# Nineteen products of the unit matrix with itself, ahead of four waits of TensorE in the first chunk of a state-space and gated feed-forward kernel

## The chip, the cores and the metric

The kernel runs on one core of a Trainium2 chip. The metric is the device time of one execution in microseconds (us). Before the change it is 373.65 us, the median of three runs (373.58 to 373.71).

## What is computed

A chunked state-space recurrence ("attention" part) gives a matrix of 3072 rows and 256 columns, and a gated feed-forward layer follows it.

```python
# attention part, per chunk of the sequence (4 batches, 8 heads, 768 positions, 32 channels, state 16)
cum = np.cumsum(la, axis=-1)                      # la: log of the clipped decays a
L = np.exp(cum[:, :, :, None] - cum[:, :, None, :]) * causal
CB = np.einsum('bhin,bhjn->bhij', Cc, Bc)
y_intra = np.einsum('bhij,bhjd->bhid', CB * L, xc)
y_inter = np.einsum('bhin,bhnd->bhid', Cc, state) * np.exp(cum)[:, :, :, None]
y[:, :, sl] = y_intra + y_inter
state = decay_full[:, :, None, None] * state + np.sum(Bx, axis=2)
# feed-forward part, on y as rows of 256
gate = 1.0 / (1.0 + np.exp(-(x @ w_gate)))        # 256 -> 1536
val = x @ w_val
out = (gate * val) @ w_out                        # 1536 -> 256
```

## The kernel before

**Tiling and stages.** The sequence of 768 positions is cut into six chunks of 128 (`NCH`), and a unit is one chunk of one of the four batches (`Unit`, and `FirstUnit` for the first chunk). A unit transposes B and C on TensorE with the unit matrix `eye` (tile `pt`, L386 and L387), takes scores of C with B (`pcb`, L464), weighs them with decays on VectorE (`m`, L478), multiplies by x (L490) and by B for the states (L497), and adds the part that comes from earlier states (L541; L624 in the first chunk). The decays of the first chunk are spread over partitions by TensorE (tile `pa`, L580) and become products along the row by a scan on VectorE (L586). When the four batches of a chunk are done, the feed-forward layer takes them together as 512 columns: gate products (`pg`), a sigmoid on ScalarE (`g`), value products (`pv`), gate times value on VectorE (`h`), then the output projection (`po`, L839 to L859). In the first chunk the first four pairs of gate and value are done in halves of 256 columns (L714), so that they can start when half of the rows exist; two more use whole float32 weights (L804). All others use weights and inputs split into a high and a low part (L813).

**Weights.** Each weight tile `wr` arrives by DMA (L304, L308) and is put into its working form by VectorE, ScalarE, VectorE, ScalarE and GpSimd in turn (`split_w`, L318 to L331).

**What sets the order.** Nothing reorders the work when the program runs: each engine's order is written out beforehand by `run()`. It keeps a list of tasks, each a generator that yields one step at a time with an engine, a cost and what it needs and makes, and picks the next step by planned starting times and by the due times of the table `DUES`. When a step is picked, the generator goes on and issues that step's instructions. On the chip each engine works through its list and waits on semaphores where its operands are not there yet. All DMAs are issued by SyncE in one order, over eight semaphore lanes in turn (`LANES = 8`), so that a transfer also waits for the one eight places ahead of it.

**The PSUM banks.** The pool `ps_mm` has three buffers of the tag `mm`, taken in turn by every tile of that tag: `pa`, `pp`, `pg`, `pv`, `po`. A tile can be written when the reader of the tile three places earlier is done.

**The start.** L126 multiplies a zero tile three times (`WARM`) before any input is there. Behind it stand the spreads `pa` of the first units, the transposes of unit 0_0 (which wait for a part of B and C), `pp`, the rest of the spreads and scores, then the transposes of 0_2 and 0_3 (the second half of the first chunk's positions), the products L490 and L497, and the first gate product `pg0_0_0`. The step names that the change uses are `products0_0`, `products0_2`, `products0_3` (L993) and `gate0_0_0` (L1023).

Of the kernel before, what the change touches and what calls it, by code (L numbers as in the profile page):

```python
# [8 lines left out]
F32 = mybir.dt.float32  # L9
# [49 lines left out]
AHEAD = 46.7  # L59
STATE = 30.0  # L60
SPARE = 1.0


W_MAX = (2.0 - 2.0**-3 - 2.0**-23) * 2.0**16
# [3 lines left out]
def tile_ssd_then_gated_ffn(  # L68
# [11 lines left out]
    nc = tc.nc  # L80
# [4 lines left out]
    P = 128  # L85
# [23 lines left out]
    ps_mm = ctx.enter_context(tc.tile_pool(name="ps_mm", bufs=3, space=PSUM))  # L109
# [20 lines left out]
    eye = const.tile([P, P], F32, name="eye")  # L130
# [34 lines left out]
    tasks = []  # L165
# [14 lines left out]
    def run():  # L180

        free = {"sp": 1.0, "pe": 1.2 + 1.7 * WARM, "act": 3.5, "dve": 6.0, "pool": 6.2, "none": 0.0}
        port_free = [0.0]
        dma_free = 0.0
        landed = [0.0] * LANES

        turns, turn_of = [0.0] * 3, {}
        made = {}
        spare = {"y": [0.0], "banks": [0.0] * 3, "cb": [0.0], "g": [0.0] * 3, "o": [0.0] * 2}
        tasks.sort(key=lambda t: t[:2])  # L190
        while tasks:
            ready_ones = []
            for n, (_, _, (eng, cost, needs, makes, port, buffers), ready, gen, name) in enumerate(tasks[:400]):
                if any(k not in made for k in needs) or any(m > len(spare[k]) for k, m in buffers.items()):
                    continue
                if buffers.get("banks") == 1:
                    if turns[-3] is None:
                        continue
                    ready = max(ready, turns[-3])
                for k, m in buffers.items():  # L200
                    ready = max([ready] + spare[k][: max(m, 0)])

                def begin(e):
                    s = max([free[e], ready] + [made[k][0] for k in needs if made[k][1] != e or e == "sp"])
                    return max(s, port_free[0]) if e == "pool" or (e == "dve" and port) else s

                if not isinstance(eng, str):
                    cost, eng = min(zip(cost, eng), key=lambda ce: begin(ce[1]) + ce[0] + SPARE * (ce[1] == "dve"))
                ready_ones.append((begin(eng), eng, n, cost))
            if not ready_ones:  # L210
                raise ValueError(f"the plan has a circle: {[t[2] for t in tasks[:20]]}")
            first = min(ready_ones, key=lambda r: r[0])

            start, eng, n, cost = next(r for r in ready_ones if r[1] == first[1] and r[0] <= first[0] + HOLD)
            t = tasks[n]
            _, _, needs, makes, port, buffers = t[2]
            end = start + cost
            if eng == "sp":

                many, end = round(cost / 0.52), start  # L220
                for _ in range(many):
                    end = max(end, landed[-LANES]) + 0.52
                    dma_free = max(dma_free, end + DMA_L) + port / many
                    landed.append(dma_free + DMA_L)
            free[eng] = end
            if eng == "pool" or (eng == "dve" and port):
                port_free[0] = end
            t[3] = end + {"pe": PE_L}.get(eng, SEM)
            if eng == "sp":
                t[3] = landed[-1]  # L230
            for k in makes:
                made[k] = t[3], eng
            if buffers.get("banks") == 1:
                turn_of[t[5]] = len(turns)
                turns.append(None)
            elif buffers.get("banks") == -1:
                turns[turn_of.pop(t[5])] = t[3]
            for k, m in buffers.items():
                spare[k] = sorted(spare[k][max(m, 0) :] + [t[3]] * -m)
            try:  # L240
                t[2] = t[4].send(eng)
            except StopIteration:
                del tasks[n]
# [774 lines left out]
    for k in range(NCH):  # L1018
# [16 lines left out]
        if k == 0:  # L1035
            t = FFN1
    run()


# [29 lines left out]
```

## Time and profile before

| what | us |
|---|---|
| median of three runs | 373.65 |
| the profiled execution | 374.85 |
| its span, from the first to the last instruction | 373.0 |
| TensorE busy in it | 360.9 |
| VectorE, ScalarE, GpSimd busy in it | 157.0, 151.1, 150.1 |

The profiled execution is one run of its own: 373.0 us of span and 1.85 us around it. The traces are read with times from the start of that span. PE is TensorE's matmuls and PEld its weight loads, which overlap them; DVE is VectorE, ACT ScalarE, POOL GpSimd, and SP or SPq SyncE, which issues the transfers. A row of the timeline merges like instructions that follow each other: start, time from the first's start to the last's end, engine, line, operation, output and inputs, count; in brackets the idle time before it and what ended that.

### The profile page before, as it was taken

What the parts mean: (1) busy time and instruction counts of PE and PEld (TensorE: products, weight loads), DVE (VectorE), ACT (ScalarE), POOL (GpSimd) and SP (SyncE); (2) the same over time, 40 slices, a digit from 0 to 9 for tenths busy, and PEclk for the clock granted to TensorE, in tenths of its full rate; (3) what the DMA queues carried; (4) which work ended last, traced back from release to release, by engine and by line L of the source; (5) the groups of instructions that cost most, each with busy time, mean ns of one, the idle gap of its engine ahead of it and who ended that gap; (6) DMA issues with size and microseconds to landing.
All of it is one profiled execution on the core that took longest, in us unless ns stands there. A gap on an engine that the chain in (4) does not pass through costs nothing.

```text
span 373.0 us, 8123 instructions
## 1 busy us (share of the span) xinstructions
PE 360.9 (97%) x3376; PEld 287.0 (77%) x3376; DVE 157.0 (42%) x277; ACT 151.1 (41%) x314; POOL 150.1 (40%) x159
## 2 busy tenths in 40 slices
PE   7788999999999999999999999999999999999996
PEld 2267668877878888888878888788877788888885
DVE  4756557768435444553354622430224440222201
ACT  2656686423575411544511245430254420254400
POOL 4425476463797520244440045430144420145410
PEclk9669999999999999999999999999999999999999
DMA  6999996527236322502332300400000000000000
GB/s 121 208 233 184 243 314 169 96 44 122 67 30 113 30 71 60 106 22 34 26 99 82 89 4 6 53 10 29 30 1 2 2 2 28 30 0 0 2 28 28
DMA packets 89270, 26.27 MB, mean 70 GB/s; under 512 B 76306, under 2 KB 82002, under 8 KB 89234
## 3 DMA queue, kind: packets, MB, share of 16 engines
q1 hardware_dynamic: 89234, 25.76, 31.8%
q8 instruction: 26, 0.43, 0.5%
q14 instruction: 10, 0.08, 0.1%
HBM read 22.41 MB, written 3.34 MB: 69 GB/s over the span
## 4 chain that ended last, share of the span: by engine, by line
PE 88%; SPq 5%; DMA 4%; POOL 1%; issue 1%; DVE 0%; ACT 0%
PE pv L813 25%; PE pg L813 24%; PE po L850 15%; PE po L851 7%; PE po L839 6%; DMA cn<-in_C_dram 2%; SPq L304 2%; PE pcb L464 2%; PE pcb L490 2%; PE pcb L541 2%; SPq L262 1%; DMA bn<-in_B_dram 1%; SPq L274 1%; PE pcb L497 1%; POOL wr L331 1%; PE pt L386 1%
## 5 line engine op out<-in xcount | busy, mean ns | idle before, releaser
L781 POOL TENSOR_TENSOR h<-g,h 128x512 fp32r<-128x512 f32 x60 | 78.5, 1308 | 126.6 <-ACT h L779 126.3
L813 PE MATMUL pv<-xh,w 128*128 128x512 f32 x264 | 93.9, 396 | 0.0
L813 PE MATMUL pg<-xh,w 128*128 128x512 f32 x264 | 93.3, 394 | 0.0
L850 PE MATMUL po<-w,h 128*128 128x512 f32 x228 | 82.1, 402 | 0.0
L775 DVE TENSOR_TENSOR g<-pv,g 128x512 f32<-128x512 f32 x60 | 41.5, 691 | 93.0 <-PE pv L813 87.5
L779 ACT CAST h<-g 128x512 fp32r<-128x512 f32 x59 | 36.6, 621 | 75.7 <-DVE g L775 75.7
L851 PE MATMUL po<-w,h 128*128 128x256 f32 x228 | 63.9, 280 | 0.0
L813 PEld LDWEIGHTS pg<-xh,w 128*128 128x128 f32 x264 | 49.6, 188 | 10.8 <-issue 0.2
L813 PEld LDWEIGHTS pv<-xh,w 128*128 128x128 f32 x264 | 49.6, 188 | 10.7 <-issue 0.3
L813 PE MATMUL pv<-xl,w 128*128 128x512 f32 x132 | 51.5, 390 | 0.0
L813 PE MATMUL pg<-xl,w 128*128 128x512 f32 x132 | 51.4, 390 | 0.0
L850 PEld LDWEIGHTS po<-w,h 128*128 128x128 f32 x228 | 42.8, 188 | 11.0 <-issue 0.5
L754 ACT ACTIVATE g<-pg 128x512 f32<-128x512 f32 x68 | 40.7, 599 | 14.7 <-PE pg L813 13.8
L851 PEld LDWEIGHTS po<-w,h 128*128 128x128 f32 x228 | 43.0, 189 | 0.2
L866 ACT COPY o<-po 128x256 f32<-128x256 f32 x20 | 7.5, 373 | 65.7 <-PE po L851 65.1
L419 DVE TENSOR_TENSOR_SCAN ab<-ab,delta 128x512 f32<-128x512 f32 x20 | 28.0, 1406 | 8.3 <-DMA ab<-a_z 8.2
L868 DVE TENSOR_TENSOR o<-po,o 128x256 f32<-128x256 f32 x20 | 8.4, 424 | 49.6 <-ACT o L866 49.5
L813 PEld LDWEIGHTS pg<-xl,w 128*128 128x128 f32 x132 | 24.8, 188 | 4.8
L813 PEld LDWEIGHTS pv<-xl,w 128*128 128x128 f32 x132 | 24.8, 188 | 4.6
L348 POOL TENSOR_TENSOR w<-wr,w 128x512 fp32r<-128x512 f32 x18 | 23.8, 1326 | 9.7 <-ACT w L346 8.8
L331 POOL TENSOR_TENSOR wr<-wr 128x512 int32<-128x512 int32 x18 | 19.6, 1091 | 20.0 <-ACT wr L329 17.9
L839 PE MATMUL po<-wr,h 128*128 128x256 f32 x96 | 23.4, 393 | 0.0
(96 smaller groups left out, 371.1 us busy)
## 6 DMA issues: line engine op xcount, KB each, us to landing
ab<-a_z SPq DMA_DIRECT2D x40, 128.0 KB
wr<-in_moe_w_val_dram SPq DMA_DIRECT2D x6, 512.0 KB
wr<-in_moe_w_gate_dram SPq DMA_DIRECT2D x6, 512.0 KB
wr<-in_moe_w_out_dram SPq DMA_DIRECT2D x6, 512.0 KB
out_dram<-o SPq DMA_DIRECT2D x24, 128.0 KB
xn<-in_x_dram SPq DMA_DIRECT2D x10, 256.0 KB
bn<-in_B_dram SPq DMA_DIRECT2D x10, 128.0 KB
cn<-in_C_dram SPq DMA_DIRECT2D x10, 128.0 KB
```

The costliest lines, as they stand in the source:

```text
L331: nc.gpsimd.tensor_tensor(out=lw.bitcast(I32), in0=hw.bitcast(I32), in1=lw.bitcast(I32), op=ALU.add)
L348: engines[eng].tensor_tensor(out=lo, in0=lw, in1=hi.bitcast(F32), op=ALU.subtract)
L419: nc.vector.tensor_tensor_scan(out=t.rearrange("p h l -> p (h l)"), data0=t.rearrange("p h l -> p (h l)"), data1=delta.rearrange("p h l -> ...
L754: nc.scalar.activation(gs[k, f], pm, AF.Sigmoid)
L775: nc.vector.tensor_tensor(out=g, in0=pm, in1=g, op=ALU.mult)
L779: copies[eng](hh, g)
L781: engines[eng].tensor_tensor(out=hl, in0=g, in1=hh.bitcast(F32), op=ALU.subtract)
L813: nc.tensor.matmul(pm, w[:, part, kt, fs], xx[:, kt], start=(i == 0), stop=(i == 3 * NK - 1))
L839: nc.tensor.matmul(acc[:, :DM], hs[k, f][:, js], whole[NF + f // 2][:, f % 2], start=start, stop=stop, skip_group_check=True,)
L850: nc.tensor.matmul(acc, hh, w.rearrange("p i m -> p (i m)"), start=start, stop=False, skip_group_check=True)
L851: nc.tensor.matmul(acc[:, :DM], hl, w[:, 0, :], start=False, stop=stop, skip_group_check=True)
L868: nc.vector.tensor_tensor(out=o, in0=acc[:, DM:], in1=o, op=ALU.add)
```

## The change

A table `FILLS` names four steps of TensorE in the first chunk. When `run()` has picked one of them, and before its instructions are issued, a tile `fill` of the pool `ps_mm` is taken and the unit matrix is multiplied by itself into its first 128 columns: 5, 6, 3 and 5 times, 19 in all. Nothing reads `fill`.

```diff
+FILLS = {"products0_0": {0: 5}, "products0_2": {0: 6}, "products0_3": {0: 3}, "gate0_0_0": {0: 5}}
...
+        nth = {}
+
+        def warm_up(many):
+
+            if many:
+                fill = ps_mm.tile([P, 512], F32, tag="mm", name="fill")
+            for _ in range(many):
+                nc.tensor.matmul(fill[:, :P], eye, eye, start=True, stop=True)
+
         tasks.sort(key=lambda t: t[:2])
...
             start, eng, n, cost = next(r for r in ready_ones if r[1] == first[1] and r[0] <= first[0] + HOLD)
+            if eng == "pe" and tasks[n][5] in FILLS:
+                name = tasks[n][5]
+                nth[name] = nth.get(name, -1) + 1
+                warm_up(FILLS[name].get(nth[name], 0))
             t = tasks[n]
```

The planner does not count the products: costs, planned times and therefore the order of all other instructions stay what they were, on TensorE and on the other four engines. Line numbers behind the added lines are higher by 14 in the changed kernel (L386 becomes L400).

On TensorE at the first place, ahead of the transposes of unit 0_0, the rows of before are these (`pt` the transposes, `pp` a product for the decays, `pa` the spreads; the names in brackets are the semaphores that an instruction waits for):

```order
L580 MATMUL pa1_140<-apart_118,of_b_102 64x512
L580 MATMUL pa2_151<-apart_118,of_b_102 64x512 [waits Pool_49]
L580 MATMUL pa2_151<-apart_118,of_b_102 64x512
L386 MATMUL pt0_0_157<-eye_88,bn0_0_126 128x128 [waits DMAHW5_49,DMAHW4_49,PE_49]
L387 MATMUL pt0_0_157<-eye_88,cn0_0_121 128x128 [waits DMAHW2_49,DMAHW1_49]
L681 MATMUL pp0_162<-early_82 128x256 [waits Pool_49]
L580 MATMUL pa3_173<-apart_118,of_b_102 64x512 [waits DVE_49]
```

And of the change:

```order
L594 MATMUL pa1_140<-apart_118,of_b_102 64x512
L594 MATMUL pa2_151<-apart_118,of_b_102 64x512 [waits Pool_49]
L594 MATMUL pa2_151<-apart_118,of_b_102 64x512
L198 MATMUL fill_157<-eye_88 128x128 x5
L400 MATMUL pt0_0_163<-eye_88,bn0_0_126 128x128 [waits DMAHW5_49,DMAHW4_49,PE_49]
L401 MATMUL pt0_0_163<-eye_88,cn0_0_121 128x128 [waits DMAHW2_49,DMAHW1_49]
L695 MATMUL pp0_168<-early_82 128x256 [waits DVE_49,Pool_49]
L594 MATMUL pa3_179<-apart_118,of_b_102 64x512 [waits DVE_49]
```

`fill` takes the third bank, so `pp` moves to the bank of `pa1` and now waits for VectorE's scan of it, and `pa3` moves to the bank of `pa2`: its wait for VectorE is now for the scan of `pa2`, where it was for the scan of `pa1`.

Ahead of the first gate product the rows of TensorE before are these (`m` the weighed scores, `xn` x, `bd` B with decays, `xw` the feed-forward input, `wr` weights):

```order
L490 MATMUL pcb0_0_180<-m0_1_245,xn0_0_146 32x64 x16
L497 MATMUL pcb0_0_180<-xn0_0_146,bd0_1_171 32x64 x8
L714 MATMUL pg0_0_0_319<-xw0_308,wr0_134 128x256 [waits DMAHW1_49,Activation_49,Pool_49]
L714 MATMUL pg0_0_0_319<-xw0_308,wr0_134 128x256
L464 MATMUL pcb0_2_330<-bct0_2_236 64x128 [waits DVE_49,PE_49]
```

And of the change:

```order
L504 MATMUL pcb0_0_186<-m0_1_258,xn0_0_146 32x64 x16
L511 MATMUL pcb0_0_186<-xn0_0_146,bd0_1_177 32x64 x8
L198 MATMUL fill_336<-eye_88 128x128 x5
L728 MATMUL pg0_0_0_342<-xw0_325,wr0_134 128x256 [waits DMAHW1_49,Activation_49,Pool_49]
L728 MATMUL pg0_0_0_342<-xw0_325,wr0_134 128x256
```

The five products stand between the state products and the gate product and wait for nothing themselves; the gate product's waits stay.

SyncE's order is the same in both. Around the transfer of C for the second chunk (`cn1_0`) it reads, before and, but for the line numbers, after:

```order
L304 DMA wr10_361<-in_moe_w_gate_dram 128x2x512 [waits DMAHW2_49]
L304 DMA wr11_371<-in_moe_w_val_dram 128x2x512 [waits DMAHW3_49]
L304 DMA wr9_378<-in_moe_w_val_dram 128x2x512 [waits DMAHW4_49]
L308 DMA wr16_430<-in_moe_w_out_dram 128x2x512 [waits DMAHW5_49]
L262 DMA bn1_0_457<-in_B_dram 128x16x16 [waits DMAHW6_49]
L262 DMA cn1_0_459<-in_C_dram 128x16x16 [waits DMAHW7_49]
```

Each of these waits for a transfer's lane alone (DMAHW), none for an arithmetic engine. Nothing moved here.

## The prediction

> **What bounds the kernel now.** I read the page first, then the stretches, then the waits of TensorE.
>
> ```profile
> span 373.0 us, 8123 instructions
> ...
> PE 360.9 (97%) x3376; PEld 287.0 (77%) x3376; DVE 157.0 (42%) x277; ACT 151.1 (41%) x314; POOL 150.1 (40%) x159
> ...
> PEclk9669999999999999999999999999999999999999
> ```
>
> TensorE is busy for 360.9 of 373.0 us. Its granted clock is low only in the second to fourth of the 40 slices. The stretches show both facts sharply; the columns are the stretch in us, its length, the busy time (and instructions) of PE, PEld, DVE, ACT and POOL, the granted clock, the DMA share and GB/s.
>
> ```profile
> 11.40:11.50 0.10, 0.10 (x4) 0.03 (x2) 0.10 (x1) 0.00 (x0) 0.10 (x1) 0.82 0.00 0
> 11.50:25.10 13.60, 9.49 (x159) 5.26 (x159) 7.94 (x15) 7.31 (x18) 5.38 (x9) 0.50 1.02 246
> 25.10:25.20 0.10, 0.10 (x2) 0.07 (x2) 0.01 (x1) 0.00 (x0) 0.10 (x1) 0.92 0.22 33
> 25.20:46.00 20.80, 18.69 (x199) 14.52 (x198) 13.10 (x30) 14.05 (x29) 9.95 (x12) 1.00 0.89 200
> 46.00:369.70 323.70, 323.70 (x2981) 263.68 (x2981) 129.75 (x218) 125.99 (x259) 129.30 (x126) 1.00 0.25 53
> 369.70:373.00 3.30, 0.04 (x1) 0.00 (x0) 0.42 (x1) 0.00 (x0) 0.00 (x0) 1.00 0.11 40
> ```
>
> From about 11.5 to 25.1 us TensorE runs at half clock. From 46.0 to 369.7 it has no idle time at full clock: 323.70 of 323.70 us. So the end is the moment at which TensorE gets past 46 us, plus a fixed amount of work. What happens earlier counts only through that moment. All its idle time before it is this:
>
> ```profile
> PE pt L386 <- DMA bn<-in_B_dram: 3.1, 2, 1.6
> PE pg L714 <- issue: 2.9, 2, 1.5
> PE warm L126 <- DVE early L123: 1.1, 1, 1.1
> PE pt L386 <- ACT bct L401: 1.0, 1, 1.0
> PE pt L387 <- DMA cn<-in_C_dram: 0.6, 1, 0.6
> ```
>
> The last row is the last wait, and in the timeline and the chain that ended last it looks like this (start, duration, engine, line):
>
> ```profile
> 45.10 0.27 PE L386 MATMUL pt<-eye,bn 128*128 128x128 f32 x1
> 45.98 0.33 PE L387 MATMUL pt<-eye,cn 128*128 128x128 f32 x1 [0.61 <-DMA cn<-in_C_dram]
> 46.15 1.89 PE L804 MATMUL pg<-xw,wr 128*128 128x512 f32 x4
> ```
>
> ```profile
> 36.63 0.56 SPq L262 DMA_DIRECT2D bn<-in_B_dram  x1
> 37.23 5.87 SPq L262 DMA_DIRECT2D cn<-in_C_dram  x1
> ```
>
> ```profile
> 37.23 8.71 DMA cn<-in_C_dram
> ```
>
> The transfer of C for the second chunk is issued from 37.23 us on and lands 8.71 us later, at 45.94; TensorE had reached it 0.61 us before. In the order of SyncE this transfer, and each one ahead of it from the weight tile wr10 on, waits only for the transfer eight places earlier. No arithmetic engine stands in that part of the queue. So 45.94 us is a floor that TensorE's speed does not move.
>
> **The change part by part.** It adds 19 products of the 128x128 unit matrix in front of four waits. The other four engines keep their instructions, order and producers. The waits, and the rows for the price of a product:
>
> ```profile
> 8.91 0.30 PE L386 MATMUL pt<-eye,bn 128*128 128x128 f32 x1 [1.52 <-DMA bn<-in_B_dram]
> ...
> 15.85 0.45 PE L386 MATMUL pt<-eye,bn 128*128 128x128 f32 x1 [1.58 <-DMA bn<-in_B_dram]
> 16.09 0.42 PE L387 MATMUL pt<-eye,cn 128*128 128x128 f32 x1
> 17.51 0.47 PE L386 MATMUL pt<-eye,bn 128*128 128x128 f32 x1 [0.99 <-ACT bct L401]
> ...
> 21.18 2.05 PE L714 MATMUL pg<-xw,wr 128*128 128x256 f32 x4 [1.44 <-issue]
> ...
> 40.58 0.27 PE L386 MATMUL pt<-eye,bn 128*128 128x128 f32 x1
> 40.69 0.27 PE L387 MATMUL pt<-eye,cn 128*128 128x128 f32 x1
> 40.79 1.03 PE L714 MATMUL pv<-xw,wr 128*128 128x256 f32 x4
> ```
>
> No product of this shape is in the trace. A float32 matmul leaves two records (L714: two matmuls, four records). The nearest rows are the two transposes of the same shape: one record each, 0.11 us apart at full clock (40.58, 40.69, 40.79) and 0.24 apart at half clock (15.85, 16.09). So I take 0.22 us for a product at full clock and 0.48 at half. The bounds come from L714: its two matmuls of 256 columns take 0.87 us at full clock (34.53 to 35.40, quoted below), 0.43 each. If the weight load and not the columns sets the pace, a product costs the same 0.43; if the columns alone do, half of it, 0.22. I take 0.22, since the transposes carry the same load.
>
> At full clock the four groups take 5, 6, 3 and 5 times 0.22, that is 1.1, 1.3, 0.7 and 1.1 us, each less than its wait (1.52, 1.58, 0.99, 1.44). Their cost is then nothing, hidden by the waits themselves; without the waits it would be 19 x 0.22 = 4.2 us. At 0.43 they take 2.2, 2.6, 1.3 and 2.2 us and stand out of the four waits by 0.7, 1.0, 0.3 and 0.8, at most 2.8 us together.
>
> A second effect is in the banks. A group takes one of three PSUM banks in turn, so the tile pa behind the first group now waits for the scan that reads the second pa, not the first:
>
> ```profile
> 9.58 1.20 DVE L586 TENSOR_TENSOR_SCAN ab<-pa,delta 128x512 f32<-128x512 f32 x1
> 9.88 0.64 PE L580 MATMUL pa<-apart,of_b 32*64 32x512 f32 x2
> ```
>
> That scan ends at 10.78, so this pa starts about 0.9 us later than 9.88. Queued behind it on TensorE are the first scores (pcb), two transposes, the fourth pa and eight more scores. The next wait, 1.58 us for the transfer that ends at 15.85, covers the 0.9.
>
> If the clock holds, the work between 11.5 and 25.1 us gets up to twice as fast. How far TensorE then leads is limited by others:
>
> ```profile
> 25.40 0.43 DVE L318 TENSOR_SCALAR wr<-wr 128x512 f32<-128x512 f32 x1 [0.29 <-DMA wr<-in_moe_w_gate_dram]
> 25.75 0.69 DVE L478 TENSOR_TENSOR m<-pcb,ab 128x512 f32<-128x512 f32 x1
> ...
> 33.17 0.41 DVE L738 TENSOR_TENSOR h<-pv,g 128x256 f32<-128x256 f32 x1
> ```
>
> ```profile
> 27.45 0.45 PE L490 MATMUL pcb<-m,xn 64*32 64x64 f32 x32
> ...
> 29.20 1.14 PE L714 MATMUL pg<-xw,wr 128*128 128x256 f32 x4
> ...
> 33.12 0.71 PE L714 MATMUL pg<-xw,wr 128*128 128x256 f32 x2 [1.50 <-issue]
> ...
> 34.53 1.03 PE L714 MATMUL pg<-xw,wr 128*128 128x256 f32 x4
> 35.40 1.03 PE L714 MATMUL pv<-xw,wr 128*128 128x256 f32 x4
> ```
>
> VectorE's second m follows a weight transfer (25.40) and ends at 25.75 + 0.69 = 26.44. The products L490 need it, so they can start at 26.5 instead of 27.45: a lead of 0.95 us. The gate product at 34.53 needs the bank that the h of 33.17 frees at 33.58, so there too it leads by at most 0.95. This also swallows the 1.50 us ahead of 33.12, which no semaphore explains. At the last wait the lead becomes waiting: TensorE arrives near 44.4, waits 1.55 instead of 0.61, and goes on at 45.98 as before.
>
> Sum against the profiled execution's own time, 374.85 us (span 373.0 and 1.85 around it): 19 products 0, the late pa 0, the faster clock 0.95 minus 0.95. That leaves 374.85. The median of the timed runs is 373.65, 1.20 less, and stays too. **Forecast: 373.65 us.**
>
> **The rivals.** *Faster: the floor is an artefact of recording.* The profiled run took 1.20 us more. If that is all transfers slowed by recording, C lands at 44.74 in a timed run, TensorE (45.37) does not wait for it, and its lead counts. It then gains 45.37 - 44.74 = 0.63 at least, 0.95 by the limit above, and 0.95 + 1.20 = 2.15 if VectorE's transfers come earlier too. I take 0.95, the row-based one: 372.7. For it: the slack is only 0.61. Against it: the three timed runs lie within 0.13 us (373.58 to 373.71), and nothing says where the 1.20 lies.
>
> The Trainium skill, "TensorE: Matmul & The Clock Gate", section "Part 1: The HAM clock gate", says that the window over which activity is judged runs freely and is not reset when a kernel starts. Half-clock stretches would then begin elsewhere in each run, and a time that hangs on TensorE's speed before 46 us would scatter; by that rule the 0.13 us speak against this rival, and no trace here shows the window itself.
>
> *Slower: the products take the place of the waits and more, because the clock does not come back.* At half clock the second group takes 6 x 0.48 = 2.9 us. TensorE starts it 0.9 late, at 15.17 instead of 14.27, and ends at 18.05 instead of 15.85. With the third (1.4) and the fourth (2.4) behind it, the first gate product starts near 24.8, 3.6 us late. Two things absorb lateness behind it: the 1.50 ahead of 33.12, if that pause passes meanwhile, and the 0.61 at the last wait. So +1.5 us, 375.15; +3.0 if the pause is not absorbed, and nothing if TensorE is less than 2.1 us late at the gate product, which is the point from which it decides. The same holds for products at 0.43 with the clock at full: at most 2.8 late, +0.7. Against it: the clock rose at 25.1, 3.9 us after the first L714 (21.18), whose work fills the array as these products do; from 15.2 it should rise near 19. If the clock simply stays as it was and the lateness is absorbed, the change does not do what it says, and the time is 373.65 all the same.
>
> *Slower: the longer last wait lowers the clock again.* A wait of 1.55 us is like the 1.52 ahead of 8.91, after which the clock fell, and like the 1.50 ahead of 33.12, after which it did not. Dense work behind would lift it sooner than after the 13.6 us seen; at a quarter of that, 3.4 us at half clock lose 1.7 us: 375.35.
>
> The Trainium skill, same page, section "Why this matters for your kernels", says that an idle gap must exceed about 3 us, one idle window, before the clock halves. By that rule this rival is empty and its chance goes to the forecast; nor would the products have anything to prevent. The trace disagrees: the clock fell at about 11.5 us and no gap ahead of it was longer than 1.6 us. So the rival keeps a chance.
>
> **How the numbers follow.** Chances: forecast 0.60; recording 0.22; late products 0.11; clock at the last wait 0.07. A measurement of this kernel tells about 0.2%, 0.75 us, from no change: 372.90 to 374.40. Of the recording case 0.16 lies below that, the rest inside; of the late products 0.06 lies above, and so does all of the last case. So faster 0.16, within 0.71, slower 0.13. For 8 in 10 the range takes the forecast, most of the recording case and the near end of the late products: 372.6 to 374.6.
>
> **What would show it.** The pt of L387 with the C transfer starts at 45.9 to 46.1 us with a wait of about 1.5 us, and no idle time follows. The low clock starts later or ends sooner. The four groups end before their transposes' transfers land. The pa at 9.88 starts near 10.8. I am wrong if the last wait is gone or shrinks, if C lands at another time, or if TensorE idles behind it.

## The result, and the profile after

The kernel with the change takes **376.72 us** (median of 7 runs, 375.57 to 378.47); the kernel before, beside it, 373.78 (373.58 to 374.74). The ratio is 1.0075, 95% interval 1.0047 to 1.0102: slower by some 2.9 us. The forecast was 373.65 with a range up to 374.6. The profiled execution took 375.74 us, its span is 374.0.

The waits of TensorE after the change (engine, line, what was waited for: total, times, longest in us; a group and a cut to its first rows):

```profile
PE pcb L478 <- issue: 2.6, 1, 2.6
PE pcb L638 <- issue: 2.2, 1, 2.2
PE warm L127 <- DVE early L124: 1.1, 1, 1.1
PE pa L594 <- DVE ab L600: 0.7, 1, 0.7
PE pt L400 <- ACT bct L415: 0.2, 1, 0.2
```

The four waits are nearly gone, and so is the wait for C. In their place stand two waits of 2.6 and 2.2 us that the view calls "issue": time for which no semaphore accounts. Before, two waits carried this name. The 1.44 ahead of 21.18, which the fourth group now fills, turns out to be an ordinary one: ScalarE's second copy of `xw`, the gate product's input, ends at 21.08 (20.71 + 0.37), and the product's weight load starts at 21.15; in banks, little4, little19, warm0 and little38 below it again ends 0.07 to 0.08 us after that copy. The 1.50 ahead of 33.12 is left. The timeline shows where they stand (start, length, number of records, idle time ahead):

```profile
7.76 1.38 PE L198 MATMUL fill<-eye 128*128 128x128 f32 x10
...
13.82 2.93 PE L198 MATMUL fill<-eye 128*128 128x128 f32 x12
...
16.97 0.96 PE L198 MATMUL fill<-eye 128*128 128x128 f32 x6
...
19.66 1.38 PE L198 MATMUL fill<-eye 128*128 128x128 f32 x10
21.17 1.11 PE L728 MATMUL pg<-xw,wr 128*128 128x256 f32 x4
22.21 0.54 PE L478 MATMUL pcb<-bct 32*64 32x128 f32 x17
25.35 0.47 PE L478 MATMUL pcb<-bct 32*64 32x128 f32 x15 [2.60 <-issue]
...
32.21 0.68 PE L638 MATMUL pcb<-cd,m 32*64 32x64 f32 x28 [2.20 <-issue]
```

```profile
46.95 0.27 PE L400 MATMUL pt<-eye,bn 128*128 128x128 f32 x1
47.06 0.27 PE L401 MATMUL pt<-eye,cn 128*128 128x128 f32 x1
```

The first pause splits a run of 32 equal scores into 17 and 15, the second a run of 32 equal products into 4 and 28: no operand begins or ends there. The transpose of C, at 45.98 before, stands at 47.06 and no longer waits. SyncE issues its transfer 1.75 us earlier than before (37.23):

```profile
35.48 5.68 SPq L276 DMA_DIRECT2D cn<-in_C_dram  x1
```

To see what the pauses have in common, take the stretches up to them (columns as in the prediction). First the kernel before, cut at its pause and at its C transpose, then the same of the kernel after:

```profile
0.00:33.10 33.10, 24.90 (x346) 14.06 (x346) 19.60 (x46) 16.48 (x37) 13.00 (x24) 0.79 0.89 191
33.10:45.95 12.85, 12.25 (x49) 9.26 (x49) 7.13 (x14) 8.65 (x19) 7.79 (x10) 1.00 0.89 208
45.95:373.10 327.15, 323.76 (x2981) 263.70 (x2981) 130.22 (x219) 125.99 (x259) 129.30 (x126) 1.00 0.25 53
```

```profile
0.00:25.30 25.30, 20.50 (x219) 12.45 (x219) 12.43 (x29) 11.19 (x26) 11.13 (x22) 0.93 0.86 193
0.00:32.20 32.20, 25.16 (x346) 16.19 (x347) 15.60 (x36) 13.40 (x30) 12.17 (x23) 0.95 0.87 196
32.20:47.05 14.85, 14.84 (x87) 11.82 (x87) 10.66 (x22) 11.12 (x25) 8.25 (x10) 1.00 0.99 248
47.05:374.10 327.05, 323.62 (x2983) 263.59 (x2981) 131.25 (x219) 126.06 (x260) 129.96 (x127) 1.00 0.24 50
```

**The count is the same.** Before its pause the old kernel has issued 346 matmuls and 346 weight loads, the new one 346 and 347, though the program stands at another place. The other pause stands at 219 and 219, together 438, which is 255 fewer than 693. With the records of TensorE's semaphores and its drain, which these columns leave out (11 up to the first pause, 12 or 13 up to the second), the pauses stand behind instruction 449 and, in both kernels, behind instruction 705: 256 apart. The page's third part has a queue that the prediction passed over (packets, MB, share of the DMA engines), before and after:

```profile
q8 instruction: 26, 0.43, 0.5%
```

```profile
q8 instruction: 27, 0.44, 0.5%
```

That is some 16 KB a packet, and one packet more with 76 instructions more. The pauses end soon after such a packet: in the trace of after they lie at 22.60 to 23.95 and 29.32 to 30.50 us and TensorE goes on at 25.35 and 32.21, that is 1.40 and 1.71 later; before, the packet of 30.46 to 31.69 is followed by 33.12, 1.43 later. The transfers of the stretch 29.25 to 30.55 us of after show the second of them:

```profile
q8 instruction: 1, 0.02, 5.6%
```

Theory 1, then: TensorE's instructions come through the DMA engines in blocks of 256, and TensorE pauses where it reaches the end of a block before the next is there. The 19 products are 76 instructions (two matmuls and two weight loads each). They put the block's end 76 instructions earlier in the program, so that more of the first chunk's work is left behind the pause. The stretches give the sum: from the end of the pause to the C transposes 12.25 us of work (49 matmuls) before, 14.84 (87) after. The pause ends 0.91 us earlier (33.12 to 32.21), the work behind it is 14.85 instead of 12.86 with the 0.61 of waiting: 1.08 us later at the C transposes. From there to the end it is 327.05 us with 323.6 to 323.8 of PE in both, as the prediction had it.

That accounts, to some 0.2 us, for the difference of the two profiled executions, 0.89 us (374.85 to 375.74). The trace of before is one of its slower runs, though. Banks below has before's instructions on TensorE, and its trace, of a run of 373.89 us, starts the C transpose at 45.08: against that one the change is 1.98 us later there and 1.85 in time.

Of the seven timed runs of the change, the three at a mean clock of 0.991 to 0.995 took 375.57 to 375.74, the four at 0.982 to 0.986 376.72 to 378.47. So within this kernel a second loss goes with the clock. Between the kernels the mean clock decides nothing: the runs of before beside the experiments have a lower one, 0.973 to 0.982, and a lower median.

The Trainium skill, "Runtime: NRT & Kernel Launch", section "Instruction fetch mechanics", states blocks of 16 KiB, 256 instructions, fetched over a DMA queue of the engine's own, and that crossing a block's end is mostly hidden. The traces agree on the 256 and disagree on the hiding: 1.5 us were open before the change and 4.8 after.

### The profile page after: what moved, and what is told of

Read it like the earlier page. It is cut to its first block, busy times and chain, and to the rows that moved or that the text cites. A ratio compares the mean times of both kernels' runs of the same rounds, so it can differ in the third digit from the quotient of the medians.

```text
span 374.0 us, 8200 instructions
## 1 busy us (share of the span) xinstructions
PE 363.6 (97%) x3414; PEld 291.6 (78%) x3414; DVE 157.5 (42%) x277; ACT 150.6 (40%) x314; POOL 150.4 (40%) x159
## 3 DMA queue, kind: packets, MB, share of 16 engines
q1 hardware_dynamic: 89234, 25.76, 31.5%
## 4 chain that ended last, share of the span: by engine, by line
PE 95%; issue 1%; DMA 1%; DVE 1%; SPq 1%; ACT 0%
PE pv L827 25%; PE pg L827 24%; PE po L864 15%; PE po L865 7%; PE po L853 6%; PE pcb L504 2%; PE pcb L478 2%; PE pg L728 2%; PE pv L728 2%; PE pcb L555 2%; PE pcb L511 1%; DMA wr<-in_moe_w_val_dram 1%; PE fill L198 1%; PE pt L400 1%; PE pg L818 1%
## 5 line engine op out<-in xcount | busy, mean ns | idle before, releaser
L362 POOL TENSOR_TENSOR w<-wr,w 128x512 fp32r<-128x512 f32 x18 | 24.7, 1378 | 9.5 <-ACT w L360 9.5
```

What stands on the lines that cost most here:

```text
L362: engines[eng].tensor_tensor(out=lo, in0=lw, in1=hi.bitcast(F32), op=ALU.subtract)
```

## The experiments

All kernels are small edits of the one before or after. "Tiny product" below is this one, read by nothing:

```
nc.tensor.matmul(
    warm[:64, :16], warm_sb[:32, :64], warm_sb[:32, :16], start=True, stop=True, skip_group_check=True
)
```

The rivals of theory 1 are that the turns of the PSUM banks make the chain late, that the products' own time does, and that the clock alone does. The table collects what came out: instructions added ahead of the gate products, pauses over 0.5 us at a block's end, when TensorE passed instruction 705 and began the C transposes in the profiled execution, and the timed median. The kernel before, in the runs beside them, had medians of 374.06 to 374.27; single runs of it lay between 372.96 and 377.34.

| kernel | added | pauses, us | past 705 | C transposes | median us | ratio, 95% interval |
|---|---|---|---|---|---|---|
| before | 0 | 1.50 | 33.12 | 45.98 | 373.78 | |
| after | 76 | 2.60, 2.20 | 32.21 | 47.06 | 376.72 | 1.0075 (1.0047 to 1.0102) |
| again | 76 | 1.71 | 33.1 | 47.90 | 376.73 (one run) | |
| banks | 0 | 1.56 | 32.68 | 45.08 | 374.11 | 1.0002 (0.9982 to 1.0022) |
| warm0 | -12 | none | 34.5 | 45.48 | 374.25 | 1.0000 (0.9979 to 1.0021) |
| little4 | 16 | 2.40 | 33.48 | 48.86 | 375.11 | 1.0040 (1.0016 to 1.0065) |
| one_each | 16 | 2.02 | 32.93 | 48.33 | 377.09 | 1.0063 (1.0034 to 1.0092) |
| wide | 28 | 4.52 | 32.45 | 49.32 | 377.87 | 1.0107 (1.0084 to 1.0130) |
| little19 | 76 | none | 31.5 | 46.39 | 374.49 | 1.0014 (0.9997 to 1.0030) |
| both12 | 124 | 0.53 | 28.27 | 43.88 | 374.52 | 1.0008 (0.9986 to 1.0030) |
| both24 | 152 | none | 30.5 | 46.01 | 374.65 | 1.0020 (1.0001 to 1.0039) |
| both19 | 152 | none | 28.3 | 43.80 | 374.12 | 1.0003 (0.9980 to 1.0027) |
| halves | 152 | none | 36.2 | 51.60 | 376.95 | 1.0094 (1.0056 to 1.0132) |
| mix | 152 | none | 33.9 | 49.34 | 377.97 | 1.0093 (1.0068 to 1.0118) |
| little38 | 152 | none | 33.8 | 49.25 | 378.25 | 1.0104 (1.0080 to 1.0127) |
| spread19 | 152 | none | 41.4 | 56.85 | 384.09 | 1.0269 (1.0245 to 1.0292) |

**again: the changed kernel a second time.** No edit.

> The changed kernel once more, for a second trace. In its first trace TensorE pauses twice without any semaphore, 2.60 us inside the scores of the third unit and 2.20 us inside the L624 products of before (L638), each time behind the same count of its instructions (449 and 705 matmuls and weight loads), and both end 1.4 to 1.7 us after a 16 KB packet of the instruction queue landed. Theory 1 (instruction blocks): the 19 products are 76 instructions ahead of these points, so TensorE runs out of instructions earlier; the two pauses are at the same two places again, 2 to 3 us each, whatever the clock does. Theory 2 (late products and banks): the products themselves stand out of their waits; the pauses are chance and move or are gone. Theory 3 (clock): the time follows the mean granted clock alone, longer where it is lower, with no pauses needed.

One of the two expected pauses came, again behind instruction 449. This time the next block was there in time at 705, and the clock fell instead. The timeline and the stretches of this run (the granted clock is the number between POOL's count and the DMA share):

```profile
27.01 0.36 PE L478 MATMUL pcb<-bct 32*64 32x128 f32 x8 [1.71 <-issue]
```

```profile
21.40:28.20 6.80, 4.97 (x130) 3.88 (x115) 2.55 (x8) 2.92 (x8) 2.38 (x4) 1.00 1.12 276
28.25:31.60 3.35, 3.35 (x10) 2.56 (x8) 2.08 (x6) 1.78 (x4) 0.10 (x1) 0.50 0.79 97
31.65:47.85 16.20, 16.20 (x189) 12.80 (x188) 11.07 (x23) 11.46 (x26) 9.05 (x11) 1.00 0.95 236
```

From 28.25 to 31.60 us TensorE has no idle time and half the clock: a stretch of 3.4 us that costs 1.7. It begins just behind the pause (25.30 to 27.01).

**banks: the four PSUM tiles taken, no product computed into them.**

```
-            for _ in range(many):
-                nc.tensor.matmul(fill[:, :P], eye, eye, start=True, stop=True)
```

> The change without its products: the four tiles of PSUM are taken in turn as with the change, nothing is computed into them, TensorE has the instructions of the kernel before. Theory 1 (TensorE's instructions come in blocks of 256; the added 76 instructions put a block's end 76 instructions earlier in the program, where more work is left behind the pause): no loss, 373.7 to 374.6 in the timed runs, one pause without a semaphore at instruction 705 in front of the L714 group that had it before, resuming near 33. Rival (the turns of the banks make pa late and the lateness is never made up): the loss stays, 376 to 377.

```profile
32.68 0.49 PE L726 MATMUL pg<-xw,wr 128*128 128x256 f32 x1 [1.56 <-issue]
```

The kernel is as fast as before, with the one pause at its old place. The turns of the banks alone cost nothing that the interval shows.

**little4: the kernel before with 4 tiny products behind the warm-up.**

```
+    for i in range(4):
+        (tiny product)
```

> The kernel before with 4 tiny products (zeros, read by nothing, 16 instructions, some 0.25 us) behind the warm-up, no other change. Theory 1: instruction 705 is what was instruction 689, about two L714 groups earlier, so about 1 to 1.7 us more work is left behind a pause that ends when its block has come (near 33 us): 374.8 to 376, and up to 377 where the clock falls at the pause. Rival (16 instructions are worth their own time): 374.0 to 374.5.

Sixteen instructions that take some 0.4 us of TensorE near 6.5 us, with the first transpose behind them at 8.87 as before (8.91), make the kernel 0.94 us slower. The pause, with the clock behind it:

```profile
33.48 0.42 PE L718 MATMUL pg<-xw,wr 128*128 128x256 f32 x1 [2.40 <-issue]
```

```profile
26.90:33.65 6.75, 4.35 (x140) 3.55 (x139) 4.34 (x14) 2.90 (x7) 1.04 (x1) 1.00 0.90 198
33.70:37.05 3.35, 3.35 (x9) 2.69 (x8) 0.76 (x2) 2.06 (x4) 1.59 (x2) 0.50 0.93 216
```

The timed runs fall into two heaps: 8 at a mean clock of 0.975 to 0.980 took 374.22 to 375.26, 4 at 0.971 to 0.972 took 376.80 to 378.51. The median was expected, the second heap too, though it reaches 1.5 us beyond the 377 that stood there; a half-clock stretch of 3.4 us is worth 0.0046 of the mean clock (3.41 x 0.5 of 374).

**one_each: one product at each of the four places** (16 instructions, the banks' turns kept).

```
-FILLS = {"products0_0": {0: 5}, "products0_2": {0: 6}, "products0_3": {0: 3}, "gate0_0_0": {0: 5}}
+FILLS = {"products0_0": {0: 1}, "products0_2": {0: 1}, "products0_3": {0: 1}, "gate0_0_0": {0: 1}}
```

> The changed kernel with one product at each of the four places instead of 5, 6, 3 and 5: the same banks taken in turn, so the late spread pa (0.7 us) stays, but only 16 instructions more than before. Theory 1: the block boundary moves by 16 instructions only; one pause as before, near 33 us, perhaps a short one near 25; time 373.7 to 374.5. Theory 2 with the banks as the cause: most of the loss stays, 375.5 to 377. Theory 3: the clock falls as before, 373.7.

A miss for theory 1, which had 373.7 to 374.5 here: four products, at most 2 us of work, lose as much as nineteen. The time is near that of the banks' rival, which banks excludes; little4 shows that 16 instructions alone have a price. Here too there are two heaps: 374.66 to 374.96 at 0.976 to 0.977, 376.07 to 378.32 at 0.971 to 0.975. In the profiled execution the pause of 2.02 us ends at 32.93 and the clock is half from 32.79 to 36.20.

**wide: the same 2432 columns in 7 products of up to 512 columns** (28 instructions).

```
-                nc.tensor.matmul(fill[:, :P], eye, eye, start=True, stop=True)
+                nc.tensor.matmul(
+                    fill[:, : wide * P].rearrange("p (r l) -> p r l", r=wide), eye,
+                    eye.rearrange("p (r l) -> p r l", r=1).broadcast_to([P, wide, P]), start=True, stop=True,
+                )
```

> The same 2432 columns of the unit matrix at the same four places, but in 7 products of 128 to 512 columns instead of 19 of 128: the same or nearly the same array time, 28 instructions instead of 76. Theory 1: both pauses get shorter or come later in the program, the time lies between the two kernels, 374.0 to 375.7. Theory 2: the products take the same time and the same banks, so the loss stays, 376 to 377. Theory 3: the same work in the waits, the same clock, so as the changed kernel, 376 to 377.

```profile
32.45 0.37 PE L643 MATMUL pcb<-cd,m 32*64 32x64 f32 x3 [4.52 <-issue]
```

```profile
0.00:32.44 32.44, 25.15 (x346) 13.26 (x347) 16.70 (x36) 13.27 (x30) 11.96 (x23) 0.92 0.86 195
```

```profile
30.60:37.35 6.75, 4.90 (x15) 3.89 (x15) 3.31 (x12) 3.37 (x7) 1.25 (x2) 0.50 0.82 159
```

The time is a miss for theory 1, which expected it between the two kernels (374.0 to 375.7). The count of 346 and 347 is there again. With the clock full from 16.9 us TensorE reaches the block's end at 27.9 and waits 4.52 us; it is let go at 32.45, hardly earlier than the slower TensorE of the kernel before (33.12), and then runs at half clock till 37.4. In this trace TensorE's lead became a longer pause.

**little19: the kernel before with 19 tiny products behind the warm-up** (76 instructions, as the change).

```
+    for i in range(19):
+        (tiny product)
```

> The kernel before with 19 very small products (32 rows, 64 columns of weights, 16 columns) behind the three warm-up products at the start: the same 76 instructions, no bank taken, next to no array time, about 1 to 1.5 us ahead of the first transposes' wait of 1.52 us. Theory 1: two pauses appear at the scores of the third unit (ending near 25.3 us) and inside the L624 products (ending near 32.2), C of the second chunk is no longer waited for at 46 us, and the time goes up by 1 to 3 us (374.8 to 376.8). Theory 2: no bank and no long product, so 373.7 to 373.9. Theory 3: the array gets no more work than before in the waits, so the clock falls as before and the time stays 373.7 to 373.9.

A miss in its time, 374.49, not slower by anything that the interval shows, and in its pauses: there is none. TensorE crossed instruction 449 at 25.25, 2.3 us earlier than before (27.51), and the next packet ran at 25.81 to 27.14, only 0.56 us later. The stretch at that time, and the corresponding one of after, from its crossing of 449 at 25.35 to its packet at 29.32 and beyond:

```profile
25.30:27.20 1.90, 1.90 (x35) 1.39 (x20) 1.13 (x3) 0.70 (x2) 1.04 (x1) 0.50 0.35 44
```

```profile
25.35:30.50 5.15, 4.66 (x127) 3.74 (x128) 3.17 (x7) 2.22 (x4) 1.04 (x1) 1.00 0.91 249
```

DMA share 0.35 against 0.91, 0.6 us from crossing to packet against 4.0. TensorE passed 705 at 31.5, early enough that the 14.84 us behind it ended at 46.39. So the number of instructions ahead doesn't set the loss; what sets it is whether the block comes in time.

This pair suggests that the traffic of the loads delays the packet, but other traces speak against the DMA share as the measure. In warm0 the packet starts 0.08 us after the crossing (29.55 to 29.63), at a share of 0.95 from there to its end; in mix it starts 4.18 us after (25.16 to 29.34), at 0.82. What delays it is not shown; a kernel with lighter loads at that place was not tried.

**warm0: the kernel before without its three warm-up products** (12 instructions fewer).

```
-    for i in range(WARM):
+    for i in range(0):
```

> The kernel before without its three warm-up products (12 instructions fewer). Theory 1: instruction 705 is what was instruction 717, three L714 groups later, so about 1.3 to 2.6 us less work is left behind the pause, which ends when the block has come, near 33 us whatever TensorE does: 372.5 to 374 if the transfer of C (43.4 to 46.2 us in the traces so far) lets it. Rival (the pause is a wait of TensorE for something in the program at that place): the pause stays in front of the same group and the time is 374 or, with the clock rising later, more.

The time is that of before, not the gain that theory 1 allowed (372.5 to 374), and no pause over 0.5 us is left at a block's end. An early transpose takes as long as one did at half clock (0.42 at 16.09, before):

```profile
9.05 0.42 PE L387 MATMUL pt<-eye,cn 128*128 128x128 f32 x1
```

Here the slower TensorE arrives at the block's end at 34.5, when the packet has landed (31.09), and nothing is lost: the prediction's reading that speed before 46 us is worth little was right, for another reason.

**both19: the change with 19 tiny products behind the warm-up**, so that 152 instructions are added and the ends of the blocks fall 152 earlier in the program.

```
+    for i in range(19):
+        (tiny product)
```

> The change with its 19 products, and 19 tiny products (76 instructions, zeros, read by nothing) behind the warm-up, so that the block ends fall 152 instructions earlier than before. Theory 1: as for 38 tiny products, no pause between 25 and 46 us, so the loss of the change is gone: 371.5 to 374.2, and the C transposes near 44 to 46 us. Rival (the products' own time, their banks, or the clock cost the 2.9 us): the loss stays or grows, 376.5 to 378.

Here are all waits of TensorE over 0.25 us, and the C transposes:

```profile
PE warm L127 <- DVE early L124: 1.1, 1, 1.1
PE pt L404 <- ACT bct L419: 0.3, 1, 0.3
PE pv L831 <- ACT g L772: 0.3, 1, 0.3
```

```profile
43.69 0.27 PE L404 MATMUL pt<-eye,bn 128*128 128x128 f32 x1
43.80 0.27 PE L405 MATMUL pt<-eye,cn 128*128 128x128 f32 x1
```

With all nineteen products and more instructions than the change, both pauses are gone, the C transposes come 3.26 us earlier than with the change, and the loss in the timed runs is gone: 374.12. This is the experiment that decides: the products and the banks are the same, the places of the blocks' ends differ, and the tiny products only add work (the first group starts at 9.54, 1.8 us later than with the change). It is no gain on before, though, and the trace is of its fastest run. Seven of its runs took 372.99 to 374.26, all at a clock of 0.989 to 0.991, the other five 374.94 to 376.63, four of them at 0.980 to 0.982; what slowed those was not seen in a trace.

**little38, halves, spread19, mix: 152 added instructions in other forms.** In order: 38 tiny products behind the warm-up of the kernel before; each of the change's products cut into two of 64 columns; a tiny product behind each of the nineteen; 7 of the nineteen and 31 tiny ones.

```
# little38
+    for i in range(38):
+        (tiny product)
# halves
-                nc.tensor.matmul(fill[:, :P], eye, eye, start=True, stop=True)
+                nc.tensor.matmul(fill[:, :64], eye, eye[:, :64], start=True, stop=True)
+                nc.tensor.matmul(fill[:, 64:P], eye, eye[:, 64:], start=True, stop=True)
# spread19
                 nc.tensor.matmul(fill[:, :P], eye, eye, start=True, stop=True)
+                (tiny product, of eye into fill)
# mix
+FILLS = {"products0_0": {0: 2}, "products0_2": {0: 2}, "products0_3": {0: 1}, "gate0_0_0": {0: 2}}
+            for _ in range(4 * many + 3 * (many == 1)):
+                (tiny product, of eye into fill)
```

> The kernel before with 38 tiny products (64x16 outputs of zeros, read by nothing, 152 instructions) behind the warm-up, none of the 19 products. Theory 1: what counts is where in the program the block ends fall, not how many instructions are added. With 152 more, instruction 705 is what was instruction 553, in the burst of products of 28 us, and its block is asked for already near 19 to 20 us instead of 27.5; the next end (961) is what was instruction 809, behind the C transposes. So no pause without a semaphore between 25 and 46 us, TensorE reaches the C transposes 1 to 1.5 us earlier than before (near 44), and the time is 372 to 374.2, although twice as many instructions are added as by the change. Rival (each added instruction costs something in itself, or each added instruction early in the program makes the pauses longer): slower, 376 to 380.

> The change with each of its 19 products cut into two products of 64 columns: the same places, the same columns, twice as many instructions (152 instead of 76). Theory 1 (what counts is where in the program the ends of TensorE's blocks of 256 instructions fall, and with 152 more they fall in the burst of products of 28 us and behind the C transposes): no pause without a semaphore between 25 and 46 us, the C transposes near 44 us, and the loss is gone: 372.3 to 374.3. Rival 1 (each added instruction lengthens the pauses): slower than the change, 377 to 380. Rival 2 (the products' own time): as the change, 376 to 378.

> The change with a tiny product (64x16 outputs, read by nothing, four instructions, some 0.06 us) behind each of its 19 products: 152 added instructions in the waits. Theory 1 with what the halves showed (a product of 64 columns costs TensorE as much as one of 128, so products also cost their own time where they outlast their wait): no pause of over 1 us without a semaphore between 25 and 46 us; the 19 tiny ones cost 1.2 us in place of the 4.2 that the halves added, so the C transposes come at 44 to 45.5 us where the clock is held: 373 to 375. Rival (the change's loss is the products' own time): 377 to 378.

> The change with 7 of its 19 products (2, 2, 1, 2) and 31 tiny products behind them (8, 8, 7, 8), so again 152 added instructions in the waits, and about 3.6 us of added work in place of 4.8. Theory 1: no pause of over 1 us between 25 and 46 us. If the clock is held, the C transposes come near 44 us and the time is 372.5 to 374, below the kernel before; if the tiny products do not hold the clock (as 38 of them in front of the chain did not), 374 to 377, by the time that the chain takes at half clock and not by a pause.

None of the four has a pause at a block's end, as theory 1 said, and all four are slow: their times were misses, and for little38, halves and spread19 slower times stood with the rivals. The traces show added work in place of pauses, most of it at half clock: in little38 the tiny products run from 6.51 to 11.96, and the first transpose starts at 13.68 (8.91 before). The stretch of little38, that of halves, and that of spread19:

```profile
10.35:30.70 20.35, 16.95 (x207) 8.84 (x207) 11.19 (x18) 8.91 (x23) 6.30 (x10) 0.50 0.98 237
```

```profile
13.35:33.75 20.40, 20.40 (x214) 17.80 (x213) 7.80 (x16) 6.58 (x16) 5.13 (x8) 0.50 0.98 220
```

```profile
11.50:38.70 27.20, 27.20 (x239) 18.09 (x238) 8.39 (x16) 8.50 (x22) 6.18 (x9) 0.50 0.92 224
```

Halves has no idle time in its 20.40 us and stays at half clock; spread19 none in 27.20. In halves a product of 64 columns cost as much as one of 128: 0.22 us at full clock. In spread19 the pairs of a product and a tiny one are 0.63 apart, so a tiny one between two products costs 0.41:

```profile
8.20 0.49 PE L198 MATMUL fill<-eye 128*128 128x128 f32 x2
8.62 0.28 PE L199 MATMUL fill<-eye 32*64 32x16 f32 x2
8.83 0.49 PE L198 MATMUL fill<-eye 128*128 128x128 f32 x2
```

So the products' own time is a real cost once it outgrows the waits. For the change itself both19 and both12, with all nineteen products and no loss that their intervals show, exclude it.

**both24 and both12: two more places for the blocks' ends.** both24 drops the first group of products and takes 24 tiny ones; both12 keeps all nineteen with 12 tiny ones (124 added).

```
# both24
-FILLS = {"products0_0": {0: 5}, "products0_2": {0: 6}, "products0_3": {0: 3}, "gate0_0_0": {0: 5}}
+FILLS = {"products0_2": {0: 6}, "products0_3": {0: 3}, "gate0_0_0": {0: 5}}
+    for i in range(24):
+        (tiny product)
# both12, with the change's FILLS
+    for i in range(12):
+        (tiny product)
```

> The change without its first group of five products, with 24 tiny products (96 instructions, read by nothing) behind the warm-up: 152 added instructions before instruction 553 of the kernel before, as with 19 tiny products and all 19 of the change, but the first transposes are not held up by 2.5 us of products. Theory 1: no pause of over 1 us without a semaphore between 25 and 46 us; the C transposes near 43.5 to 44.5 us where the clock is held, and 372.3 to 373.7; at half clock in the first chunk 374 to 376. Rival (the 152 instructions helped only because of the first group's products): a pause of 2 us or more, 376 to 378.

> The change with 12 tiny products (48 instructions) behind the warm-up: 124 added instructions. Theory 1: instruction 705 is what was instruction 581, still in the burst of products of 28 us, and its block is asked for some 28 instructions of the burst of 19 us later than with 152; so as there no pause of over 1 us, the C transposes near 43.5 to 44.5 us where the clock is held, 372.5 to 375 over all runs. Rival (only the sum of the added work counts): between the change and 152 added instructions, 375 to 376.7.

```profile
28.27 0.25 PE L508 MATMUL pcb<-m,xn 64*32 64x64 f32 x2 [0.53 <-issue]
```

Both are near the kernel before, with no pause over 0.53 us, which is what both19 had shown. Neither beats it. both24's median is 0.6 us above before and above the 372.3 to 373.7 that was expected with the clock held; it ran at half clock from 9.3 to 22.9 us, and for that case 374 to 376 stood there.

## Why the prediction was wrong

- **What bounds the kernel.** Right in that nothing is lost behind the first 46 us: the stretch from the C transposes on was 327.15 us before and 327.05 after. Wrong in "45.94 us is a floor that TensorE's speed does not move". SyncE's order is the same after the change, but its times are not: it issues that transfer from 35.48 on, where it was 37.23. The transpose of C then starts without waiting, at 47.06, and in both19 (issue at 35.55) at 43.80. Nor is the landing one value without the change: in banks the transpose starts at 45.08, 0.15 us after TensorE reached it. That the last wait is gone is among the signs that the prediction named for being wrong. A smaller misreading: the page's clock row is low in the second and third slice, not up to the fourth; nothing hangs on it.
- **The price of the products.** Right: 0.22 us at full clock. The ten records from 7.76 on start 0.11 apart; at half clock those from 14.20 on are 0.21 apart, so 0.42 a product where 0.48 was taken. The reason that the prediction gives for the lower bound, "if the columns alone do", is out: in halves 64 columns cost the same 0.22.
- **The four groups hidden in their waits.** Right for the first, third and fourth, nearly so for the second (2.93 us at half clock). pa waits 0.7 us for the scan, where 0.9 was reckoned, and is covered.
- **The step that failed** is "This also swallows the 1.50 us ahead of 33.12, which no semaphore explains". The pause was taken for slack that could absorb a lead or a lateness. It is the end of an instruction block: its place in the program moves when instructions are added, and in wide it grew to 4.52 us when TensorE came earlier. The runs showed, in its place, a pause of 2.20 at the same count of instructions, a second one of 2.60 a block earlier, and 2.59 us more work behind the later one (14.84 less 12.25). "19 products 0" held for their time and left out their 76 instructions, which move the blocks' ends; little19, with 76 as well, met its blocks in time and lost nothing that its interval shows.
- **The rivals.** The recording case is out: the kernel got slower, and recording did not cost 1.2 us in banks, whose recorded run took 373.89 with a median of 374.11. The 0.13 us of scatter that spoke against it were luck of three runs (372.96 to 377.34 in the later ones). "Late products" named slower times, 375.15 and, with the pause not absorbed, 376.65, beside the 376.72 measured. That is a coincidence: the first gate product starts at 21.17 against 21.18 before, so the groups did not make it late, and banks and both19 exclude the mechanism. "The clock falls again" was right in kind and placed wrongly: it falls behind the pauses at the blocks' ends (28.25 in again, 33.70 in little4, 30.60 in wide), not at the wait for C, which is gone; its 3.4 us at half clock, worth 1.7, are what again and little4 show.
- **What stays open.** How the 2.9 us of the timed runs divide between the blocks' ends and the clock. The three runs at the higher clock are some 1.9 us above the median of before, as the trace of after is above that of banks (1.85), which speaks for 1.9 from the blocks' ends and the rest from the clock; but the slower timed runs have no trace, and again, at 0.982, is the one trace like them. Why the packet starts 0.6 us after the crossing in one run and 4.0 in another. And what slows five of both19's runs.

## What to carry to other kernels

Idle time that a profile puts down to "issue" is not slack. Look first for a producer that ends just before it ends, as ScalarE's copy did at 21.08. If there is none, count the engine's instructions up to it; if it stands at the same count in kernels with different programs, and behind a packet of the instruction queue, it is an instruction block that came late. Then every instruction added ahead, however cheap, moves that place, and so does every one removed; price it by the work between the old and the new place, and look at where the next ends fall. And a wait filled to hold the clock is worth only what the first later limit leaves of it, here a packet of instructions.

## What the runs showed of the hardware that was not expected

- TensorE pauses at the end of an instruction block. In all eight traces with such a pause over 0.5 us it stands at 449 to 450 or 705 to 706 of TensorE's instructions, and ends 1.34 to 1.71 us after a packet of the instruction queue has landed (before 1.43, after 1.40 and 1.71, again 1.34, one_each 1.52, wide 1.46, banks 1.42, little4 1.45, both12 1.44). A packet takes 0.9 to 2.1 us under the loads of this kernel.
- The clock changes at edges some 3.41 us apart, whose place differs in each execution: before, it changed at 4.64, 11.46 and 25.12 us (2 and 4 times 3.41), after, at 6.99, 13.82 and 17.23. With the edges continued from the last change, at the pauses behind 20 us it fell where one such stretch held 1.71 us of a pause (again, 24.82 to 28.23), 1.88 (one_each), 2.40 (little4) or 2.65 (wide), and not where it held 1.30 and 1.33 (after) or 1.44 (banks). The Trainium skill, "TensorE: Matmul & The Clock Gate", section "Why this matters for your kernels", has about 3 us of idle time for such a fall; these runs show it from 1.71 on. And idle time is not all that counts: in spread19 the clock fell at 11.46 us behind a stretch (8.05 to 11.46) in which TensorE had none.
- Being busy did not by itself raise the clock: in the traces, in which the ends of matmuls are modelled, halves kept TensorE without idle time for 20.40 us at half clock, spread19 for 27.20. In that time halves runs its products of 64 columns and spread19 its pairs, beside the chain's products of 32 and 64 rows; in both the clock rose only when the gate products of 128 rows and 256 columns had begun (28.85 us, risen at 33.80, in halves; 34.33 and 38.77 in spread19).
